# Replanning a two-engine split: LayerNorm work and evictions that may go to either VectorE or ScalarE, with new scheduler constants

## The chip, the cores and the metric

The kernel runs on one core of one Trainium2 chip. The metric is the device time of one execution in microseconds (us). TensorE (PE in the profile) does matmuls, VectorE (DVE) and ScalarE (ACT) do element-wise work and copy PSUM to SBUF ("evictions"), GpSimd (POOL) small things, SyncE (SP) issues DMA.

## The reference, cut to what matters

One block on x of 2048 positions × 512 features, bf16: a modulated LayerNorm; sliding, dilated local attention (32 heads of 16, window 8, dilation 2) with a residual; a second modulated LayerNorm; a third LayerNorm and an MLP *along the positions* (2048 → 1792 → 2048) with a residual.

```python
h = layernorm(x) * (1 + ca) + sa
x = x + ga * attention(h, wqkv, wo)
h = layernorm(x) * (1 + cb) + sb
u = gelu(einsum('bsd,sf->bdf', layernorm(h), w1) + b1)
x = x + gb * (einsum('bdf,fs->bds', u, w2) + b2).transpose(0, 2, 1)
```

The MLP mixes positions, so its first matmul needs the third LayerNorm, `h3`, of *every* position before it can end, and the second matmul needs all of the first.

## The kernel before

Positions come in 4 chunks of 512, each of 4 tiles of 128. A chunk goes: statistics of x, normalise (`n_sb`), transpose (`hT`), project (`q`, `k`, `v`), multiply q by shifted k (`prod`), softmax, multiply by v (`pv`), output projection plus x (`xx`), statistics, normalise (`h`), affine, statistics again (`st6c`), normalise into `h3`. The first MLP matmul runs in levels: chunks 0 and 1, then chunk 2, then chunk 3, the partial sums parked in SBUF in between. They are parked in the buffer of the projection weights, so the last projection must be over first.

The program is not written in execution order. It is a graph of operations, each with a modelled duration, and a list scheduler in Python orders it once, at build time. Some operations carry alternatives, and the scheduler picks the engine. The kernel stamps this order on the instructions, and in the traces each engine ran *its* list in it (e5 below shows an eviction between two normalisations because that is where it stood).

```python
class _Graph:
    XLAT = 0.12            # modelled hand-over between two engines, us
    ...
    def schedule(self):
        ...
            for i in avail:
                o = ops[i]
                fin = [(max(ready_time(o, e), eng_free.get(e, 0.0)) + d, e, d) for (e, d, _) in o.alts]
                best_fin = min(fin)[0]
                for f_, e, d in fin:
                    if f_ <= best_fin + 0.05:
                        per_eng.setdefault(e, []).append((f_ - d, o, d))
        ...
def copy2(dst, src_fn, n, bf16_src, ...):     # evictions: hT, lsb, a2sb, o_sb, parked MLP sums
    alts = [("act", _t_act(n), fa)]
    if FLEX:
        alts.append(("dve", (0.12 + 0.00052 * n) if bf16_src else _t_tt1(n), fd))
    return G.add_any(alts, ...)
# fixed before: statistics of x and h -> VectorE; normalise x -> VectorE;
# normalise h, evict q/k/v, evict xx with its statistics -> ScalarE
add("dve", 0.72, f, reads=[("xx", st)], writes=[("mv", b, sl)], name=f"ln1s{st}")
# ... cut
order = G.schedule()
for o in order:
    o.fn()
```

## Time and profile before

256.71 us, median of 6 runs (256.01 to 258.49). The head of the profile's page: busy time by engine, then the span in 40 slices of 6.35 us (busy tenths; PEclk is the clock that TensorE was granted).

```profile
span 254.0 us, 3475 instructions
PE 211.2 (83%) x1295; PEld 93.2 (37%) x1295; DVE 178.0 (70%) x271; ACT 125.0 (49%) x234; POOL 5.8 (2%) x32
PE   0199946994889735787879989999999999999993
DVE  2479998999999999979997798627820044444543
ACT  2035645653687854658774758887696500000000
PEclk9999997999599985589999999999999999999999
```

VectorE is full from 16 to about 130 us while TensorE has holes; from about 131 us TensorE is full. The windows view has the same in us: window, its length, then busy time (and instructions) of each engine, the granted clock, and at the end the share and the GB/s of the DMA engines.

```profile
60.00:80.00 20.00, 15.54 (x120) 7.11 (x117) 19.40 (x29) 13.33 (x29) 0.00 (x0) 0.83 0.73 99
80.00:100.00 20.00, 12.09 (x85) 4.53 (x83) 19.44 (x25) 12.42 (x21) 0.90 (x2) 0.83 0.43 63
131.50:170.00 38.50, 37.71 (x238) 15.18 (x238) 28.00 (x41) 26.83 (x58) 0.00 (x0) 1.00 0.64 125
170.00:201.00 31.00, 30.99 (x144) 13.84 (x142) 11.58 (x23) 21.97 (x37) 0.00 (x0) 1.00 0.46 133
```

The order of columns is PE, PE weight load, DVE, ACT, POOL. And some groups of instructions (engine, operation, output <- input, shapes, count | busy us, mean ns of one):

```profile
L140 DVE TENSOR_SCALAR n_sb<-xx,mv,rs 128x512 bf16<-128x512 bf16 x16 | 5.8, 406 | 0.2 <-ACT rs L140 0.2
L140 ACT ACTIVATE h<-xx,nb,rs 128x512 bf16<-128x512 bf16 x16 | 11.7, 803 | 0.9 <-DVE nb L140 0.9
L140 ACT ACTIVATE q_sb<-psA,bqkv 128x512 bf16<-128x512 f32 x16 | 10.9, 683 | 4.3 <-PE psA L140 4.3
L140 ACT ACTIVATE xx<-psW 128x512 bf16<-128x512 f32 x16 | 9.5, 594 | 6.9 <-PE psW L140 6.9
```

The three ScalarE lines have two, one and no per-partition pointer operands (scale or bias read from a column in SBUF): 803, 683, 594 ns; the first also reads bf16 from SBUF, where the others read f32 from PSUM. So ScalarE pays twice what VectorE pays for a normalisation, but less for a plain f32 eviction (`o_sb`: 593 against 687 ns; the bf16 eviction `hT` is the other way round, 592 against 417).

Last, three moments, from the timeline (start, length): the first MLP matmul, the last normalisation into `h3`, and the first matmul of the second MLP product (MLP2). How many instructions are merged into one line depends on the window that was asked for.

```profile
131.53 1.02 PE L140 MATMUL psA<-h,wst 128*128 128x512 bf16 x4 [0.72 <-ACT v_c L140]
183.57 2.92 ACT L140 ACTIVATE h<-h,nb,rs 128x512 bf16<-128x512 bf16 x4
201.35 3.84 PE L140 MATMUL psA<-wg,wst 128*128 128x512 bf16 x17 [0.36 <-DMA wst<-in_B_w_dram]
```

### The profile page before, as it was taken

How to read it: one execution, taken by the hardware profiler on the slowest of the kernel's cores; microseconds unless marked ns; L12 is line 12 of the kernel's file. 1: busy time of each engine (PE TensorE's matmuls, PEld its weight loads, DVE VectorE, ACT ScalarE, POOL GpSimd, SP SyncE). 2: the span in 40 equal slices, each digit the busy share in tenths (PEclk: the TensorE clock that was granted, in tenths of full speed). 3: DMA queues.
4: the chain of work that ended last, by engine and by line, in shares of the span. 5: the costliest groups of instructions: out<-in, count | busy, mean ns of one | idle time of the engine just before them, and what ended most of it. 6: DMA issues, size and time to landing. Idle time of an engine off the chain costs nothing.

```text
span 254.0 us, 3475 instructions
## 1 busy us (share of the span) xinstructions
PE 211.2 (83%) x1295; PEld 93.2 (37%) x1295; DVE 178.0 (70%) x271; ACT 125.0 (49%) x234; POOL 5.8 (2%) x32
## 2 busy tenths in 40 slices
PE   0199946994889735787879989999999999999993
PEld 0164413441344311243423433444444444444441
DVE  2479998999999999979997798627820044444543
ACT  2035645653687854658774758887696500000000
POOL 4000000010000100000000000000000000000000
PEclk9999997999599985589999999999999999999999
DMA  6994069796950049800009993122444966666311
GB/s 236 383 306 152 0 118 218 167 166 115 146 78 0 3 89 141 106 4 0 0 0 165 147 271 89 41 83 83 126 124 122 278 202 203 203 205 200 120 41 41
DMA packets 46596, 32.87 MB, mean 129 GB/s; under 512 B 2036, under 2 KB 45556, under 8 KB 46580
## 3 DMA queue, kind: packets, MB, share of 16 engines
q1 hardware_dynamic: 45984, 31.60, 53.8%
q10 hardware_dynamic: 596, 1.06, 1.1%
q8 instruction: 10, 0.16, 0.3%
q14 instruction: 6, 0.05, 0.1%
HBM read 22.03 MB, written 2.10 MB: 95 GB/s over the span
## 4 chain that ended last, share of the span: by engine, by line
PE 59%; DVE 17%; DMA 14%; issue 4%; ACT 3%; SPq 1%; ACTq 0%; DVEq 0%; POOLq 0%
PE psA L140 43%; DVE pv L140 7%; PE psT L140 7%; PE psW L140 4%; DMA wst<-in_B_w_dram 4%; DMA b_t<-in_B_b_dram 4%; DMA vD<-v_c 4%; DMA wst<-in_w_mod_dram 2%; ACT h L140 2%; PE psO L140 2%; PE psL L140 2%; DVE h L140 2%; DVE prod L140 1%; SPq L140 1%; PE psX L140 1%
## 5 line engine op out<-in xcount | busy, mean ns | idle before, releaser
L140 PEld LDWEIGHTS <-wst 128*128 128x128 bf16 x448 | 43.1, 98 | 56.4 <-issue 3.7
L140 PE MATMUL psA<-hT,wg 128*128 128x512 bf16 x192 | 49.1, 398 | 3.0 <-ACT v_c L140 1.2
L140 PE MATMUL psA<-wg,wst 128*128 128x512 bf16 x224 | 48.5, 379 | 0.4 <-DMA wst<-in_B_w_dram 0.4
L140 DVE SCALAR_TENSOR_TENSOR h<-psA,b2col,gb_bc 128x512 f32<-128x512 f32 x16 | 12.0, 751 | 41.1 <-PE psA L140 41.1
L140 PE MATMUL psA<-h,wst 128*128 128x512 bf16 x152 | 37.8, 380 | 1.5 <-DMA wst<-in_B_w_dram 0.8
L140 DVE TENSOR_TENSOR pv<-a2sb,vD 128x2048 bf16<-128x2048 bf16 x32 | 37.7, 1217 | 0.0
L140 DVE TENSOR_TENSOR prod<-q_sb,k_c 128x4096 bf16<-128x4096 bf16 x16 | 36.0, 2285 | 0.4 <-PE psL L140 0.4
L140 PEld LDWEIGHTS <-wg 128*128 128x128 bf16 x240 | 23.2, 117 | 28.5 <-issue 12.5
L140 PE MATMUL psW<-woq,o_sb 128*128 128x512 bf16 x64 | 20.0, 443 | 0.9 <-ACT xx L140 0.8
L140 PE MATMUL psO<-pv,stack 128*32 128x512 bf16 x128 | 12.3, 432 | 8.9 <-DVE pv L140 6.2
L140 PE MATMUL psT<-h,wst 128*128 128x512 bf16 x72 | 18.0, 380 | 0.0
L140 DVE BATCH_NORM_STATS2 st<-xx 128x6 f32<-128x512 bf16 x16 | 10.7, 672 | 4.5 <-DMA xx<-in_A_x_dram 4.5
L140 PE MATMUL psL<-prod,group 128*32 128x512 bf16 x128 | 9.9, 398 | 4.8 <-DVE prod L140 4.8
L140 ACT ACTIVATE v_c<-psA,bqkv 128x512 bf16<-128x512 f32 x16 | 10.8, 685 | 6.0 <-PE psA L140 5.8
L140 ACT ACTIVATE k_c<-psA,bqkv 128x512 bf16<-128x512 f32 x16 | 10.9, 681 | 5.2 <-PE psA L140 5.2
L140 ACT ACTIVATE q_sb<-psA,bqkv 128x512 bf16<-128x512 f32 x16 | 10.9, 683 | 4.3 <-PE psA L140 4.3
L140 ACT ACTIVATE xx<-psW 128x512 bf16<-128x512 f32 x16 | 9.5, 594 | 6.9 <-PE psW L140 6.9
L140 ACT ACTIVATE h<-h,nb,rs 128x512 bf16<-128x512 bf16 x16 | 11.7, 801 | 2.0 <-DVE nb L140 2.0
L140 ACT ACTIVATE h<-xx,nb,rs 128x512 bf16<-128x512 bf16 x16 | 11.7, 803 | 0.9 <-DVE nb L140 0.9
L140 ACT ACTIVATE o_sb<-psO 128x512 bf16<-128x512 f32 x11 | 6.5, 593 | 11.2 <-PE psO L140 11.2
L140 DVE TENSOR_TENSOR h<-h,xx 128x512 bf16<-128x512 f32 x16 | 11.1, 692 | 0.6
L140 PE MATMUL psT<-ident,n_sb 128*128 128x128 bf16 x64 | 7.2, 271 | 4.4 <-DVE n_sb L140 3.1
(94 smaller groups left out, 200.2 us busy)
## 6 DMA issues: line engine op xcount, KB each, us to landing
vD<-v_c SPq DMA_DIRECT2D x64, 130.0 KB, 5.0
wst<-in_B_w_dram SPq DMA_DIRECT2D x8, 896.0 KB, 4.9
wst<-in_B_w_dram SPq DMA_DIRECT2D x7, 512.0 KB, 5.3
wst<-in_B_w_dram SPq DMA_DIRECT2D x14, 256.0 KB, 2.8
xx<-in_A_x_dram SPq DMA_DIRECT2D x4, 512.0 KB, 11.0
wst<-in_w_mod_dram SPq DMA_DIRECT2D x4, 512.0 KB, 6.1
out_dram<-h SPq DMA_DIRECT2D x16, 128.0 KB, 1.7
wg<-in_A_wqkv_dram SPq DMA_DIRECT2D x1, 1536.0 KB, 9.4
```

What stands on the lines that cost most here:

```text
L140: r = fn(*a, **k)
```

## The change

The intent is to take work off VectorE: LayerNorm statistics, normalisations and projection evictions get an alternative on the other engine, and the scheduler adds 1 us to VectorE's finish time when it compares the two. The modelled hand-over goes from 0.12 to 0.3 us. Four small groups of start-up operations are moved by hand after the scheduling, and four weight loads go to GpSimd's DMA queue.

```diff
-    XLAT = 0.12
+    XLAT = 0.3                 # (set from the argument XLAT = 30)
+    EBIAS = {}                 # (set to {"dve": 1.0} from DBIAS = 100)
-                best_fin = min(fin)[0]
+                best_fin = min(f_ + self.EBIAS.get(e, 0.0) for f_, e, d in fin)
                 for f_, e, d in fin:
-                    if f_ <= best_fin + 0.05:
+                    if f_ + self.EBIAS.get(e, 0.0) <= best_fin + 0.05:
# ...
+    def ln_stats(...):         # bn_stats on VectorE, or on ScalarE:
+        def fa():
+            # with eviction
+            nc.scalar.activation(evac_dst, x, ACT.Identity, accum_out=sums_ap[:, 0:1])
+            nc.scalar.activation(mv_ap[:, 0:1], sums_ap[:, 0:1], ACT.Identity, scale=1.0 / D)
+            nc.scalar.activation(junk[:], evac_dst, ACT.Square, scale=-1.0, bias=mv_ap[:, 0:1],
+                                 accum_out=mv_ap[:, 1:2])
+            # ... (without eviction: the same in another order)
+        alts = [("dve", d_dve, fd), ("act", d_act, fa)] if FLEX else [("dve", d_dve, fd)]
+    def ln_norm(...):          # tensor_scalar on VectorE, or activation on ScalarE
+        alts = [("dve", _t_ts(D), fd), ("act", _t_act(D, 2), fa)] if FLEX else [("act", _t_act(D, 2), fa)]
# ... q/k/v evictions: [("act", ...)] + [("dve", _t_tt1(C), fdv)]
# ... one small VectorE op per chunk (nb1) added before the first normalisation, three (mean, msq, ve) removed
+                q=nc.gpsimd if li == 0 and fc >= NWS else None)
# ...
     order = G.schedule()
+    move(("modcols", "modcols_cp"), "ln1n3")
+    move(("tr0_0", "hT0_0", "hT0_1", "tr0_1"), "modcols", before=True)
+    move(("biascols", "biascols_cp"), "w_scale")
+    move(("hT0_2", "hT0_3"), "tr0_1")
```

More of the change, by code (lines that the diff above doesn't have):

```diff
@@ L126, in schedule @@
         return order
+_CUR = [None]
 class _EngProxy:
@@ L143, in wrapped @@
                 self._tc.stamp_issue_order_token(ins, self._token)
+                if _CUR[0] and hasattr(r, "annotate"):
+                    r.annotate(_CUR[0])
             return r
@@ L210 @@
     FLEX: int = 1,
+    DBIAS: int = 100,
+    XLAT: int = 30,
 ):
@@ L214 @@
     G.WIN = WIN / 100.0
+    G.EBIAS = {"dve": DBIAS / 100.0}
+    G.XLAT = XLAT / 100.0
     SB = C // 4
@@ L309 @@
     sums = [T([P, TPC, 2], F32, f"sums{i}") for i in range(2)]
-    mean2 = [T([P, TPC], F32, f"mean2_{i}") for i in range(2)]
-    msq2 = [T([P, TPC], F32, f"msq2_{i}") for i in range(2)]
-    ve2 = [T([P, TPC], F32, f"ve2_{i}") for i in range(2)]
+    sums1 = [T([P, TPC, 2], F32, f"sums1_{i}") for i in range(2)]
+    sums3 = [T([P, TPC, 2], F32, f"sums3_{i}") for i in range(2)]
+    nb1 = [T([P, TPC], F32, f"nb1_{i}") for i in range(2)]
+    st6b = [T([P, TPC, 6], F32, f"st6b_{i}") for i in range(2)]
+    mv2 = [T([P, TPC, 2], F32, f"mv2_{i}") for i in range(2)]
     lv2 = [T([P, TPC], F32, f"lv2_{i}") for i in range(2)]
@@ L339, in copy2, with dma, ln_stats, fd @@
         return G.add_any(alts, reads=reads, writes=writes, name=name)
-    def dma(out_ap, in_ap, nbytes, reads, writes, name):
-        return add("sp", 0.65, lambda: nc.sync.dma_start(out_ap, in_ap), reads=reads, writes=writes, name=name,
+    def dma(out_ap, in_ap, nbytes, reads, writes, name, q=None):
+        return add("sp", 0.65, lambda: (q or nc.sync).dma_start(out_ap, in_ap), reads=reads, writes=writes, name=name,
                    bytes_=nbytes)
+    def ln_stats(src_fn, evac_dst, st6_ap, mv_ap, sums_ap, reads, writes, name):
+        def fd():
+            x = src_fn()
+            if evac_dst is not None:
+                nc.vector.tensor_copy(evac_dst, x)
+                x = evac_dst
+            nc.vector.bn_stats(st6_ap, x)
+            nc.vector.bn_aggr(mv_ap, st6_ap)
+            if evac_dst is not None:
+                nc.vector.tensor_scalar(mv_ap[:, 1:2], mv_ap[:, 1:2], float(D), None, op0=ALU.mult)
+        def fa():
+            x = src_fn()
+            if evac_dst is not None:
+                nc.scalar.activation(evac_dst, x, ACT.Identity, accum_out=sums_ap[:, 0:1])
+                nc.scalar.activation(mv_ap[:, 0:1], sums_ap[:, 0:1], ACT.Identity, scale=1.0 / D)
+                nc.scalar.activation(junk[:], evac_dst, ACT.Square, scale=-1.0, bias=mv_ap[:, 0:1],
+                                     accum_out=mv_ap[:, 1:2])
+            else:
+                nc.scalar.activation(junk[:], x, ACT.Identity, scale=1.0 / D, accum_out=mv_ap[:, 0:1])
+                nc.scalar.activation(junk[:], x, ACT.Square, scale=-1.0, bias=mv_ap[:, 0:1], accum_out=sums_ap[:, 1:2])
+                nc.scalar.activation(mv_ap[:, 1:2], sums_ap[:, 1:2], ACT.Identity, scale=1.0 / D)
+        d_dve = 0.72 + (_t_tt1(D) if evac_dst is not None else 0.0)
+        d_act = 2 * _t_act(D) + 0.2 + 0.75
+        alts = [("dve", d_dve, fd), ("act", d_act, fa)] if FLEX else [("dve", d_dve, fd)]
+        return G.add_any(alts, reads=reads, writes=list(writes), name=name)
@@ L345, with ln_norm, fd, fa @@
+    def ln_norm(dst, src, mean_ap, rs_ap, nb_ap, reads, writes, name):
+        def fd():
+            nc.vector.tensor_scalar(dst, src, mean_ap, rs_ap, op0=ALU.subtract, op1=ALU.mult)
+        def fa():
+            nc.scalar.activation(dst, src, ACT.Identity, scale=rs_ap, bias=nb_ap)
+        alts = [("dve", _t_ts(D), fd), ("act", _t_act(D, 2), fa)] if FLEX else [("act", _t_act(D, 2), fa)]
+        return G.add_any(alts, reads=reads, writes=writes, name=name)
     G.pk = -20.0
@@ L467, in build_mod_rows, with rstd @@
         mod_row(5, 2, lambda ps: nc.vector.tensor_copy(gb_bc[:], ps[:]), "gb", 0.7, ["gb_bc"])
-    def rstd(var_ap, lv_t, rs_t, eps, reads, key, name):
+    def rstd(var_ap, lv_t, rs_t, eps, reads, key, name, scale=1.0):
         def f():
-            nc.scalar.activation(lv_t[:], var_ap, ACT.Ln, bias=epscol[:, 0:1] if eps else 0.0)
+            nc.scalar.activation(lv_t[:], var_ap, ACT.Ln, scale=scale, bias=epscol[:, 0:1] if eps else 0.0)
             nc.scalar.activation(rs_t[:], lv_t[:], ACT.Exp, scale=-0.5)
@@ L482, in build_chunk @@
             st = ch * TPC + sl
-            def f(st=st, sl=sl):
-                nc.vector.bn_stats(st6[b][:, sl, :], xx[:, st, :])
-                nc.vector.bn_aggr(mv[b][:, sl, :], st6[b][:, sl, :])
-            add("dve", 0.72, f, reads=[("xx", st)], writes=[("mv", b, sl)], name=f"ln1s{st}")
+            ln_stats(lambda st=st: xx[:, st, :], None, st6[b][:, sl, :], mv[b][:, sl, :], sums1[b][:, sl, :],
+                     [("xx", st)], [("mv", b, sl)], f"ln1s{st}")
         rstd(mv[b][:, :, 1], lv1[b], rs1[b], True, [("mv", b, sl) for sl in range(TPC)] + ["consts"], ("rs1", b),
              f"rstd1_{ch}")
+        add("dve", 0.12, lambda: nc.vector.scalar_tensor_tensor(nb1[b][:], mv[b][:, :, 0], -1.0, rs1[b][:],
+                                                               op0=ALU.mult, op1=ALU.mult),
+            reads=[("rs1", b)] + [("mv", b, sl) for sl in range(TPC)], writes=[("nb1", b)], name=f"ln1b{ch}")
         for sl in range(TPC):
             st = ch * TPC + sl
-            def f(st=st, sl=sl):
-                nc.vector.tensor_scalar(n_sb[b][:, sl, :], xx[:, st, :], mv[b][:, sl, 0:1], rs1[b][:, sl:sl + 1],
-                                        op0=ALU.subtract, op1=ALU.mult)
-            add("dve", _t_ts(D), f, reads=[("xx", st), ("rs1", b), ("mv", b, sl)], writes=[("n_sb", 0, sl)],
-                name=f"ln1n{st}")
+            ln_norm(n_sb[b][:, sl, :], xx[:, st, :], mv[b][:, sl, 0:1], rs1[b][:, sl:sl + 1], nb1[b][:, sl:sl + 1],
+                    [("xx", st), ("rs1", b), ("nb1", b), ("mv", b, sl)], [("n_sb", 0, sl)], f"ln1n{st}")
         G.pk = (ch - 1) * 100 + RK[4] + 1
@@ L548, in f, with fdv @@
                     nc.scalar.activation(v_c[b][:, j, PAD:PAD + C], psA[a][:, 0:C], ACT.Identity, bias=bqkv[:, g:g + 1])
-            add("act", _t_act(C, 1), f, reads=[("psA", a), "bqkv"], writes=[(("q", "k", "v")[t], b, j)],
-                name=f"ev{ch}_{t}{j}")
+            def fdv(t=t, j=j, a=a):
+                g = 4 * t + j
+                dst = (q_sb[b][:, j, :], k_c[b][:, j, PAD:PAD + C], v_c[b][:, j, PAD:PAD + C])[t]
+                if t == 0:
+                    nc.vector.tensor_scalar(dst, psA[a][:, 0:C], DH ** -0.5, bqkv[:, g:g + 1], op0=ALU.mult, op1=ALU.add)
+                else:
+                    nc.vector.tensor_scalar(dst, psA[a][:, 0:C], bqkv[:, g:g + 1], None, op0=ALU.add)
+            alts = [("act", _t_act(C, 1), f)] + ([("dve", _t_tt1(C), fdv)] if FLEX else [])
+            G.add_any(alts, reads=[("psA", a), "bqkv"], writes=[(("q", "k", "v")[t], b, j)], name=f"ev{ch}_{t}{j}")
         if ch == 0:
@@ L659, in build_chunk @@
                 writes=["psW"], name=f"wo{st}")
-            def f(sl=sl, st=st):
-                nc.scalar.activation(xx[:, st, :], psW[:], ACT.Identity, accum_out=sums[b][:, sl, 0:1])
-                nc.scalar.activation(junk[:], xx[:, st, :], ACT.Square, scale=float(D) ** -0.5,
-                                     accum_out=sums[b][:, sl, 1:2])
-            add("act", 2 * _t_act(D) + 0.2, f, reads=["psW"], writes=[("xx", st), ("sums", b, sl), "junk"],
-                name=f"x1ev{st}")
-        def f():
-            nc.vector.tensor_scalar(mean2[b][:], sums[b][:, :, 0], 1.0 / D, None, op0=ALU.mult)
-            nc.vector.tensor_tensor(msq2[b][:], mean2[b][:], mean2[b][:], op=ALU.mult)
-            nc.vector.scalar_tensor_tensor(ve2[b][:], sums[b][:, :, 1], EPS, msq2[b][:], op0=ALU.add, op1=ALU.subtract)
@@ L672, in build_chunk @@
-        add("dve", 0.3, f, reads=[("sums", b, sl) for sl in range(TPC)], writes=[("ve2", b)], name=f"ln2a{ch}")
-        rstd(ve2[b][:], lv2[b], rs2[b], False, [("ve2", b)], ("rs2", b), f"rstd2_{ch}")
-        add("dve", 0.12, lambda: nc.vector.scalar_tensor_tensor(nb2[b][:], mean2[b][:], -1.0, rs2[b][:], op0=ALU.mult,
-                                                               op1=ALU.mult),
-            reads=[("rs2", b), ("ve2", b)], writes=[("nb2", b)], name=f"ln2b{ch}")
+            ln_stats(lambda: psW[:], xx[:, st, :], st6b[b][:, sl, :], mv2[b][:, sl, :], sums[b][:, sl, :],
+                     ["psW"], [("xx", st), ("mv2", b, sl)], f"x1ev{st}")
@@ L677, in build_chunk @@
+        rstd(mv2[b][:, :, 1], lv2[b], rs2[b], True, [("mv2", b, sl) for sl in range(TPC)], ("rs2", b), f"rstd2_{ch}",
+             scale=1.0 / D)
+        add("dve", 0.12, lambda: nc.vector.scalar_tensor_tensor(nb2[b][:], mv2[b][:, :, 0], -1.0, rs2[b][:],
+                                                               op0=ALU.mult, op1=ALU.mult),
+            reads=[("rs2", b)] + [("mv2", b, sl) for sl in range(TPC)], writes=[("nb2", b)], name=f"ln2b{ch}")
         for sl in range(TPC):
             st = ch * TPC + sl
-            add("act", _t_act(D, 2),
-                lambda sl=sl, st=st: nc.scalar.activation(h2[b][:, sl, :], xx[:, st, :], ACT.Identity,
-                                                          scale=rs2[b][:, sl:sl + 1], bias=nb2[b][:, sl:sl + 1]),
-                reads=[("xx", st), ("nb2", b), ("rs2", b)], writes=[("h2", b, sl)], name=f"t{st}")
+            ln_norm(h2[b][:, sl, :], xx[:, st, :], mv2[b][:, sl, 0:1], rs2[b][:, sl:sl + 1], nb2[b][:, sl:sl + 1],
+                    [("xx", st), ("nb2", b), ("rs2", b), ("mv2", b, sl)], [("h2", b, sl)], f"t{st}")
@@ L689, in build_chunk @@
         for sl in range(TPC):
-            def f(sl=sl):
-                nc.vector.bn_stats(st6c[b][:, sl, :], h2[b][:, sl, :])
-                nc.vector.bn_aggr(mv3[b][:, sl, :], st6c[b][:, sl, :])
-            add("dve", 0.72, f, reads=[("h2", b, sl)], writes=[("mv3", b, sl)], name=f"ln3s{ch}_{sl}")
+            ln_stats(lambda sl=sl: h2[b][:, sl, :], None, st6c[b][:, sl, :], mv3[b][:, sl, :], sums3[b][:, sl, :],
+                     [("h2", b, sl)], [("mv3", b, sl)], f"ln3s{ch}_{sl}")
         rstd(mv3[b][:, :, 1], lv3[b], rs3[b], True, [("mv3", b, sl) for sl in range(TPC)], ("rs3", b), f"rstd3_{ch}")
@@ L699, in build_chunk @@
             st = ch * TPC + sl
-            add("act", _t_act(D, 2),
-                lambda sl=sl, st=st: nc.scalar.activation(h3[:, st, :], h2[b][:, sl, :], ACT.Identity,
-                                                          scale=rs3[b][:, sl:sl + 1], bias=nb3[b][:, sl:sl + 1]),
-                reads=[("h2", b, sl), ("nb3", b), ("rs3", b)], writes=[("h3", st)], name=f"h3_{st}")
+            ln_norm(h3[:, st, :], h2[b][:, sl, :], mv3[b][:, sl, 0:1], rs3[b][:, sl:sl + 1], nb3[b][:, sl:sl + 1],
+                    [("h2", b, sl), ("nb3", b), ("rs3", b), ("mv3", b, sl)], [("h3", st)], f"h3_{st}")
     for ch_ in range(NCH):
@@ L734 @@
             w1p = wst[w][:, 0:nst, :]
-            dma(w1p, w1_view[:, s_lo:s_hi, fc * EW:(fc + 1) * EW], P * nst * EW * 2, [], [("wst", w)], f"ld_w1_{li}_{fc}")
+            dma(w1p, w1_view[:, s_lo:s_hi, fc * EW:(fc + 1) * EW], P * nst * EW * 2, [], [("wst", w)], f"ld_w1_{li}_{fc}",
+                q=nc.gpsimd if li == 0 and fc >= NWS else None)
             for fl in range(EW // P):
@@ L794, with move @@
     order = G.schedule()
+    def move(names, anchor, before=False):
+        nonlocal order
+        ops_ = [o for o in order if o.name in names]
+        order = [o for o in order if o.name not in names]
+        at = next(i for i, o in enumerate(order) if o.name == anchor) + (0 if before else 1)
+        order[at:at] = ops_
+    move(("modcols", "modcols_cp"), "ln1n3")
+    move(("tr0_0", "hT0_0", "hT0_1", "tr0_1"), "modcols", before=True)
+    move(("biascols", "biascols_cp"), "w_scale")
+    move(("hT0_2", "hT0_3"), "tr0_1")
     if DUMP:
@@ L801 @@
     for o in order:
+        _CUR[0] = o.name if DUMP else None
         o.fn()
+    _CUR[0] = None
 _INS = ['A_x', 'A_wqkv', 'A_wo', 'B_x', 'B_w1', 'B_b1', 'B_w2', 'B_b2', 'c', 'w_mod']
```

## The prediction

> **What bounds the kernel now.** The windows view splits the 254.0 us span into three. (1) To 15.8 us: start-up, waiting for loads. The first projection runs at 16.5 us. (2) 16 to 131.5 us: attention, where VectorE is busy 22.9 of 24.2, 18.3 of 20, 19.4 of 20, 19.4 of 20, 17.6 of 19.9 and 11.4 of 11.6 us. ScalarE is busy only 12.4, 11.7, 13.3, 12.4, 13.8, 9.4 there, TensorE about 90 of 115. The MLP cannot start before the last projection (its buffer is reused) and h3 of the second chunk; its first matmul is at 131.5 us. (3) From 131.5 us to the end TensorE is saturated (37.7 of 38.5, 31.0 of 31.0, 48.5 of 53 with the output tail). So the time is set by when TensorE saturates, and that is VectorE's queue in stage 2.
>
> **What the change does.** It lets the static scheduler put LayerNorm statistics, normalisations and projection evictions on either engine, and handicaps VectorE by 1 us in the choice. From the groups by form: a statistic costs VectorE 0.80 us of pace (0.67 + 0.18, overlapped) and would cost ScalarE about 1.9 us (0.6 + 0.63 plus two accumulator reads of 0.19 and a small op of 0.2: an estimate from the post-attention statistics). A normalisation costs 0.34 us against 0.73 us. The Trainium skill, "ScalarE: Activation LUTs" (What ACT_TABLE_LOAD costs) puts about 93 ns on each per-partition pointer operand; the trace agrees: 0.59, 0.685, 0.80 us with none, one, two.
>
> In stage 2 some 24 us of VectorE work can move (12 statistics of x, 12 normalisations, up to 8 statistics of h, about 15 evictions). ScalarE has about 35 us idle and pays about twice as much. Balance comes near 10 to 12 us moved. Waits between the two engines eat some; I count 7 us of earlier saturation. TensorE must do the same work in less time; its idle there (about 25 us) suffices, and fewer gaps may remove part of the half-clock stretches (mean clock 0.75 to 0.83 between 60 and 120 us).
>
> Start-up: transposes move ahead of the column matmuls, bias columns behind them. The chain is still the 1 MB w_mod load (about 11.7 us), column matmuls, bias matmuls, weight scaling, projection: 0.5 us gained. Four w1 loads leave the blocked SP queue for GpSimd's: it removes the 0.76 us wait at 150.5 us, no more. Stage 3 keeps its matmuls (MLP2 48.5 us unchanged), and the chunk tails (normalise, affine, statistics, h3) shorten, so saturation should hold.
>
> **Predicted: 248 us, range 241 to 254.5.** Faster by over 2%: 0.70; within 2%: 0.25; slower: 0.05.
>
> **What would show it.** First MLP matmul near 124 us instead of 131.5; VectorE total down from 178 to about 165, ScalarE up from 125 to about 150; statistics and normalisations appearing as ScalarE activations in the groups; first projection near 16 us; time from first MLP matmul to end unchanged within 2 us; clock nearer 1 between 60 and 120 us.
>
> **What would make it wrong.** ScalarE statistics of 1.9 us sit in order in front of projection evictions, and with two projection banks TensorE then stalls, so ScalarE becomes the new limiter. TensorE could get gaps in stage 3 if chunk 3's h3 (ready at 186.5 us, used from 186 us) does not come earlier by as much as the rest. The GpSimd-issued loads could land late beside VectorE ("SBUF - State Buffer" of the skill, on the shared port); no run here shows that yet.

## The result, and the profile after

250.13 us, median of 8 runs (249.49 to 251.34), against 257.97 us for the kernel before over 16 runs. The ratio is 0.9716, 95% interval 0.9687 to 0.9744. Ratios here are the mean time of one kernel's runs over that of the other's in the same rounds, so not quite the ratio of the medians quoted. The profiled execution of before was the fastest of its 16 (256.01 us), that of after an ordinary one (249.84), so the profiles show 6.0 of the 7.8 us. The page after:

```profile
span 248.0 us, 3499 instructions
PE 209.5 (84%) x1295; PEld 91.3 (37%) x1295; DVE 166.0 (67%) x239; ACT 146.3 (59%) x297; POOL 11.6 (5%) x36
PE   0389976998989235996889999999899999999992
DVE  2369999899999998899955899116700044444442
ACT  5576577859875778797996788768876300000000
PEclk9999995899999957797999999999999999999998
```

VectorE lost 12.0 us of work and ScalarE gained 21.3 us. Most of the 12.0 is not LayerNorm work. In the groups, VectorE's plain evictions (`hT`, `o_sb`, `a2sb`, `lsb`, the parked sums), which could change engine before too, go from 27 with 17.0 us to 13 with 8.7 us. Of the new alternatives, 8 of the 32 statistics of x and h and 6 of the 16 normalisations of x left VectorE, but 6 normalisations of h, one eviction of `xx` with its statistics and two projection evictions came to it. The three moments after:

```profile
127.64 3.62 PE L144 MATMUL psA<-h,wst 128*128 128x512 bf16 x16
177.66 1.51 ACT L144 ACTIVATE h<-h,nb,rs 128x512 bf16<-128x512 bf16 x2
194.63 9.67 PE L144 MATMUL psA<-wg,wst 128*128 128x512 bf16 x44 [0.47 <-DMA wst<-in_B_w_dram]
```

The last `h3` ends 7.3 us earlier (186.5 to 179.2 us), and MLP2 starts 6.7 us earlier. The first MLP matmul moved by only 3.9 us.

There is a new hole. In the windows view, after, TensorE does 8.6 us of work between 80 and 100 us, where it did 12.1 before:

```profile
60.00:80.00 20.00, 18.95 (x147) 8.12 (x143) 19.59 (x23) 15.17 (x33) 1.00 (x1) 1.00 0.57 87
80.00:100.00 20.00, 8.61 (x68) 2.82 (x67) 18.16 (x32) 16.32 (x32) 0.98 (x1) 0.73 0.74 100
```

The timeline shows what TensorE waited for first: the eviction of `o_sb`, which stood in ScalarE's list behind the eviction of logits, four normalisations and a `v` eviction.

```profile
85.80 0.98 PE L144 MATMUL psO<-pv,stack 128*32 128x512 bf16 x8 [4.71 <-ACT o_sb L144]
80.42 1.00 ACT L144 ACTIVATE lsb<-psL 128x1024 bf16<-128x1024 f32 x1
81.76 2.93 ACT L144 ACTIVATE h<-xx,nb,rs 128x512 bf16<-128x512 bf16 x4 [0.34 <-DVE nb L144]
84.59 0.67 ACT L144 ACTIVATE v_c<-psA,bqkv 128x512 bf16<-128x512 f32 x1
85.17 0.58 ACT L144 ACTIVATE o_sb<-psO 128x512 bf16<-128x512 f32 x1
```

Over the two windows together TensorE does the same work as before, 27.6 us: what it gains in the first is given back in the second, to a queue that is longer now. Is the relief of VectorE what paid at all?

### The profile page after: what moved, and what is told of

Read it like the earlier page. It is cut to its first block, busy times and chain, and to the rows that moved or that the text cites. A ratio compares the mean times of both kernels' runs of the same rounds, so it can differ in the third digit from the quotient of the medians.

```text
span 248.0 us, 3499 instructions
## 1 busy us (share of the span) xinstructions
PE 209.5 (84%) x1295; PEld 91.3 (37%) x1295; DVE 166.0 (67%) x239; ACT 146.3 (59%) x297; POOL 11.6 (5%) x36
## 4 chain that ended last, share of the span: by engine, by line
PE 63%; DVE 21%; ACT 8%; DMA 3%; issue 3%; DVEq 0%; ACTq 0%
PE psA L144 44%; PE psW L144 7%; PE psT L144 6%; DVE pv L144 6%; DVE prod L144 4%; ACT h L144 3%; DVE h L144 3%; PE psL L144 2%; PE psO L144 2%; DMA wst<-in_B_w_dram 2%; PE psX L144 2%; DVE st6c L144 2%; DVE st L144 1%; DMA xx<-in_A_x_dram 1%; ACT junk L144 1%
## 5 line engine op out<-in xcount | busy, mean ns | idle before, releaser
L144 PE MATMUL psA<-hT,wg 128*128 128x512 bf16 x192 | 52.6, 417 | 6.4 <-DVE k_c L144 2.2
L144 PE MATMUL psA<-h,wst 128*128 128x512 bf16 x152 | 37.1, 380 | 0.0
L144 PE MATMUL psO<-pv,stack 128*32 128x512 bf16 x128 | 11.4, 425 | 9.7 <-ACT o_sb L144 6.1
L144 PE MATMUL psW<-woq,o_sb 128*128 128x512 bf16 x64 | 18.3, 409 | 0.3 <-ACT o_sb L144 0.3
L144 PE MATMUL psT<-ident,n_sb 128*128 128x128 bf16 x64 | 6.9, 268 | 10.4 <-ACT n_sb L144 6.6
L144 ACT ACTIVATE junk<-xx,mv 128x512 bf16<-128x512 bf16 x19 | 13.7, 722 | 0.6
L144 ACT ACTIVATE k_c<-psA,bqkv 128x512 bf16<-128x512 f32 x15 | 10.2, 679 | 4.7 <-PE psA L144 4.5
L144 DVE CAST wg<-psA 128x512 bf16<-128x512 f32 x6 | 4.1, 680 | 10.8 <-PE psA L144 10.7
L144 ACT ACTIVATE h<-xx,nb,rs 128x512 bf16<-128x512 bf16 x14 | 10.3, 802 | 1.4 <-DVE nb L144 1.4
L144 DVE BATCH_NORM_STATS2 st<-xx 128x6 f32<-128x512 bf16 x12 | 8.0, 670 | 4.4 <-DMA xx<-in_A_x_dram 4.4
L144 PEld LDWEIGHTS <-n_sb 128*128 128x128 bf16 x64 | 5.4, 121 | 12.8 <-ACT n_sb L144 7.0
```

The lines of the kernel that those rows point to most:

```text
L144: r = fn(*a, **k)
```

## The experiments

Three theories. **Theory 1**, the prediction's: the LayerNorm work that left VectorE is the gain. **Theory 2**: the scheduler's constants are the gain, and the new alternatives are not needed. **Theory 3**: every edit makes the scheduler draw another order for everything, and the order is the gain, whatever VectorE's total. All outputs were correct. Times are medians of 4 runs in experiments 1 to 8 and of 6 in 9 to 12; the kernel before was at 257.26, 257.32 and 257.28 us in the three groups of four. Submitted together: e1 to e4, e5 to e8, e9 to e12; each ratio is against before in the same rounds, while after was timed in rounds of its own.

### e1: the two constants alone, on the kernel before

```diff
-    XLAT = 0.12
+    XLAT = 0.3
+    EBIAS = {"dve": 1.0}      # and used in the choice, as in the change; nothing else
```

> The kernel before, with only the scheduler's two constants of the change: hand-over latency 0.3 us instead of 0.12, and the 1 us handicap of VectorE for the evictions that could already go to either engine. No LayerNorm statistic, normalisation or projection eviction may move. Theory 1 (the gain is VectorE work moved by the new alternatives): VectorE total stays near 175 us and the time within 2 us of before, 255 to 258 us. Theory 2 (the new scheduler constants alone do it, the alternatives are not needed): 248 to 252 us, VectorE total down by 5 to 8 us through evictions alone. Theory 3 (any new static order shifts the time by a few us): anything between 250 and 260, with no relation to VectorE's total.

Measured: 250.97 us, ratio 0.9749 (0.9715 to 0.9782). VectorE's total is 167.9 us: 24 evictions went from VectorE to ScalarE, 6 the other way. Almost the whole gain is there without one line of the new alternatives: the interval overlaps that of the change (0.9687 to 0.9744). The time is that of Theory 2; VectorE's relief is larger than the 5 to 8 us I expected.

```profile
PE 210.3 (84%) x1295; PEld 91.7 (37%) x1295; DVE 167.9 (67%) x253; ACT 132.9 (53%) x252; POOL 9.7 (4%) x32
```

### e2: the hand-over constant alone

```diff
-    XLAT = 0.12
+    XLAT = 0.3
```

> The kernel before with only the hand-over latency of the plan at 0.3 us. VectorE's work is the same to within 2 us. Theory 1: within 2 us of before. Theory 2: faster by 2 to 5 us[...]. Theory 3: a shift either way; the plan's own end is 13 us later than that of before (259.8 against 246.6), so if the plan is now true the kernel is slower, 256 to 262 us.

Measured: 268.71 us, ratio 1.0424 (1.0382 to 1.0466), with VectorE at 178.9 us, the work of before. A more careful constant alone made it 11 us slower, outside every range that I had written. Part of that is in waits of TensorE for w1, of which before had 0.8 us: in the group of the first MLP product 8.7 us of idle, 5.5 us of it for those loads.

```profile
L140 PE MATMUL psA<-h,wst 128*128 128x512 bf16 x152 | 39.9, 396 | 8.7 <-DMA wst<-in_B_w_dram 5.5 <-ACT h L140 3.2
```

### e3: the change without its new alternatives

```diff
-        alts = [("dve", d_dve, fd), ("act", d_act, fa)] if FLEX else ...   # statistics
+        alts = [("act", d_act, fa)] if evac_dst is not None else [("dve", d_dve, fd)]
# normalisations: x on VectorE, h on ScalarE; q/k/v evictions: ScalarE only
```

> The kernel after, with the new alternatives taken back: statistics of x and h on VectorE, normalisation of x on VectorE, of h on ScalarE, post-attention eviction and statistics and projection evictions on ScalarE, as before. Handicap, latency, start-up moves, GpSimd queue and the new form of the variance stay. Theory 1: the gain goes, 254 to 258 us, with VectorE's total back to 172 or more. Theory 2: the gain stays, 248 to 252 us. Theory 3: either, unrelated to VectorE's total.

Measured: 254.41 us, ratio 0.9879 (0.9845 to 0.9912). It lies between: taking the alternatives away from the change costs 4.3 us of its median, though e1, which never had them, is at 251.0. VectorE: 170.1 us. e3 and e1 have the same constants and the same fixed engines for the LayerNorm work; they differ in the start-up moves, the GpSimd loads and the form of the variance, and are 3.4 us apart. So edits that move little work can shift the time by nearly as much as the alternatives.

### e4: the change without the handicap

```diff
-    DBIAS: int = 100,
+    DBIAS: int = 0,
```

> The kernel after with the handicap of VectorE at 0 instead of 1 us; the alternatives stay. Theory 1: the scheduler already spreads work by finish time, so most of the gain stays, 249 to 253 us, but VectorE's total is higher than after's 166. Theory 2: the gain goes, 255 us or more, with VectorE's total above 175 us as it takes evictions and normalisations from ScalarE.

Measured: 261.33 us, ratio 1.0148 (1.0108 to 1.0189). VectorE's total rises to 190.6 us. The alternatives without the handicap *load* VectorE, because most of the operations that may now move are modelled shorter there, and the kernel is 4 us slower than before.

### e5 and e6: the engines alone, and the order alone

These two split e1. In e5 the order of before is kept, and after the scheduling 30 evictions are put on the engine that e1 chose. In e6 the order of e1 is kept, and the same 30 are put back.

```diff
     order = G.schedule()
+    for o in order:
+        want = 'act' if o.name in (24 names) else 'dve' if o.name in (6 names) else None   # e6: swapped
+        for (ae, ad, afn) in o.alts:
+            if ae == want:
+                o.eng, o.dur, o.fn = ae, ad, afn
```

> The order of instructions of before, kept as it is; only the engine of 30 evictions is changed in place, to the engines that the plan of e1 chose (24 from VectorE to ScalarE, 6 the other way). Theory 1a (the relief of VectorE is the gain, whatever the order): most of e1's gain is there, 251 to 254 us, VectorE near 168 us. Theory 3 (the order is the gain): within 2 us of before, 255 to 259 us.

> The order of e1, kept as it is; only the engines of the same 30 evictions are put back in place to what they were before. Theory 1a: the gain goes, 255 us or more, VectorE near 178. Theory 3: the gain stays, 250 to 253 us.

Measured: e5 259.54 us, ratio 1.0080 (1.0034 to 1.0127); e6 257.44 us, ratio 1.0002 (0.9972 to 1.0033). VectorE's totals were 167.6 and 177.2 us (e5, then e6):

```profile
PE 213.8 (83%) x1295; PEld 93.7 (37%) x1295; DVE 167.6 (65%) x253; ACT 132.5 (52%) x252; POOL 6.7 (3%) x32
PE 211.8 (83%) x1295; PEld 92.1 (36%) x1295; DVE 177.2 (69%) x271; ACT 123.6 (48%) x234; POOL 9.9 (4%) x32
```

e5 is just above Theory 3's range and e6 is in Theory 1a's: e5 refutes the relief alone and e6 the order alone. This is the sharpest result: taking 10.4 us off VectorE with the order kept is worth nothing (it is slightly slower), the new order with the old engines is worth nothing, and both together, in e1, are worth 2.5%.

Where part of e5's relief went can be read. The waits view of VectorE (who waited for whom, total us, times, longest), before and then e5:

```profile
DVE h L140 <- ACT h L140: 0.2, 1, 0.2
DVE h L140 <- ACT h L140: 7.5, 4, 4.0
```

One instance of the four, a short one (1.3 us; the longest, 4.0 us, is in chunk 3's tail at 178 us), before: ScalarE does four normalisations of `h` in a row, meanwhile VectorE evicts `o_sb` and goes on to the affine step at 85.67 us.

```profile
82.71 2.93 ACT L140 ACTIVATE h<-xx,nb,rs 128x512 bf16<-128x512 bf16 x4 [0.68 <-DVE nb L140]
84.79 0.68 DVE L140 CAST o_sb<-psO 128x512 bf16<-128x512 f32 x1
85.67 1.22 DVE L140 TENSOR_TENSOR h<-h,ab_bc 128x2048 bf16<-128x2048 bf16 x1 [0.20 <-ACT h L140]
```

In e5 the eviction sits on ScalarE, between the third and the fourth normalisation, since that is where it stood in the common order. VectorE is idle for it, and its affine step starts at 86.25 us, *later*:

```profile
82.81 2.22 ACT L140 ACTIVATE h<-xx,nb,rs 128x512 bf16<-128x512 bf16 x3 [0.68 <-DVE nb L140]
84.94 0.57 ACT L140 ACTIVATE o_sb<-psO 128x512 bf16<-128x512 f32 x1
85.42 0.80 ACT L140 ACTIVATE h<-xx,nb,rs 128x512 bf16<-128x512 bf16 x1
86.25 1.22 DVE L140 TENSOR_TENSOR h<-h,ab_bc 128x2048 bf16<-128x2048 bf16 x1 [1.27 <-ACT h L140]
```

### e7: the order of after, with the LayerNorm work put back

The same loop on the kernel after: statistics, normalisations and projection evictions on the engines of before, order and plain evictions kept.

> The order of after, kept as it is; only the statistics, normalisations and projection evictions are put back in place on the engines that they had before; the plain evictions stay where after has them. Some 19 items of VectorE work, about 11 us, come back. Prediction's step (the LayerNorm work moved off VectorE is what is gained): 4 to 8 us slower than after, 254 to 258 us. If the plain evictions and the order carry the gain: within 2 us of after, 248 to 252 us.

Measured: 259.13 us, ratio 1.0072 (1.0037 to 1.0106): 9.0 us slower than after's median, beyond the 4 to 8 us expected. But VectorE's total is 169.1 us: 3.1 us came back, not about 11, since the put-back returns work to both engines.

```profile
PE 209.5 (82%) x1295; PEld 90.8 (35%) x1295; DVE 169.1 (66%) x249; ACT 134.8 (52%) x264; POOL 21.7 (8%) x36
```

So of the 12.0 us that left VectorE, 3.1 us net belong to the new alternatives, and a loss of 9.0 us cannot be VectorE's load alone. Within *this* order the new alternatives are worth all of the gain. With e3 (4.3 us when the scheduler may plan again without them) this suggests how to value a part: an order fits the engines that it was planned for. One thing blurs e7: GpSimd's small copy of the k halo, which the next chunk's products read, took 11.7 us there instead of 1.4, while VectorE ran two-input multiplications back to back. First after, then e7:

```profile
50.91 1.38 POOL L144 COPY k_c<-k_c 128x64 bf16<-128x64 bf16 x1 [15.89 <-ACT k_c L144]
```

```profile
53.55 11.73 POOL L144 COPY k_c<-k_c 128x64 bf16<-128x64 bf16 x1 [17.17 <-ACT k_c L144]
56.82 8.03 DVE L144 TENSOR_TENSOR pv<-a2sb,vD 128x2048 bf16<-128x2048 bf16 x7
```

How much of the 9.0 us that is was not separated.

### e8: the handicap alone, on the kernel before

> The kernel before with only the handicap of VectorE of 1 us, the latency of the plan left at 0.12 us. If the handicap is the part that works: 249 to 253 us, as e1. If the two constants work only together: 255 us or more. The plan's own end is 242.9 us[...].

The edit is e1's without the XLAT line. Measured: 252.10 us, ratio 0.9798 (0.9767 to 0.9830). So the handicap alone brings most of it, and the hand-over constant, which alone cost 4.2%, cost nothing once the handicap was there. Three pairs differ in the handicap alone, and it paid in each: from before to e8 VectorE loses 10.6 us and the time 5.2; from e2 to e1 11.0 and 17.7; from e4 to after 24.6 and 11.2. Where the scheduler plans the order together with the relief, relief and gain go together; their sizes do not.

### e9: the change without its start-up moves

```diff
-    move(("modcols", "modcols_cp"), "ln1n3")
-    move(("tr0_0", "hT0_0", "hT0_1", "tr0_1"), "modcols", before=True)
-    move(("biascols", "biascols_cp"), "w_scale")
-    move(("hT0_2", "hT0_3"), "tr0_1")
```

> The kernel after without the four start-up moves (transposes ahead of the column matmuls, bias columns behind the weight scaling). Prediction: they are worth 0.5 us, so 0.2 to 1 us slower than after, with the first projection at 16.7 instead of 16.2 us. Rival: the order behind the start-up absorbs it and nothing changes, within 0.3 us.

Measured: 252.56 us, ratio 0.9818 (0.9791 to 0.9844), 2.4 us slower than after's median and 2.0 us slower than e10 of the same rounds; my 0.2 to 1 us was too little. The timeline of VectorE in e9 shows why:

```profile
12.28 0.17 DVE L144 COPY b1col<-psO 128x14 f32<-128x14 f32 x1 [4.92 <-PE psO L144]
12.78 0.15 DVE L144 SCALAR_TENSOR_TENSOR nb<-mv,rs 128x4 f32<-128x4 f32 x1
```

The new plan had put the bias columns' copy, which waits for a load, in front of the operation (`nb`) that ScalarE's first normalisation needs; VectorE's own first ones follow it at 12.85 us. VectorE stood 4.9 us, and the first projection ran at 17.7 us. Against the kernel before (16.5 us) the moves gain 0.3 us; against the *new* plan they repair 1.5 us.

### e10: the four loads back on the SP queue

```diff
-                q=nc.gpsimd if li == 0 and fc >= NWS else None)
+                q=None)
```

> The kernel after with the four w1 loads back on the SP queue. Prediction: they save one wait of TensorE of some 0.8 us, so 0.5 to 1.5 us slower than after. Rival: the loads of the third chunk pair wait for slots in front of the vD loads or behind them in the SP queue, and TensorE stalls longer, 2 us or more. Or: no difference, if the loads were early enough.

Measured: 250.56 us, ratio 0.9747 (0.9709 to 0.9785), which overlaps after's interval. The wait comes back in the group of the first MLP product (0.9 us, after: none), but the time does not resolve it.

```profile
L144 PE MATMUL psA<-h,wst 128*128 128x512 bf16 x152 | 37.1, 379 | 0.9 <-DMA wst<-in_B_w_dram 0.9
```

### e11 and e12: other plans for the same work

If the order matters this much, one can look for a better one. I replayed each candidate's order off the chip: every engine in its order, modelled durations, a hand-over of 0.12, 0.2 and 0.3 us, and averaged the three ends. Over the first ten measured kernels that replay at 0.2 us was off by 4 us (standard deviation) with a correlation of 0.69, so it only serves to choose; the chip decides. Of about 3,400 settings, two from the top:

```diff
# e11, against after                      # e12, against after
-    WIN: int = 25,                       # RK=(10, 20, 30, 40, 5): next chunk's LayerNorm and
+    WIN: int = 10,                       #   projections ahead of the rest in rank
-    LEVELS=(2, 3),                       # LEVELS=(1, 2, 3)
+    LEVELS=(1, 2, 3),                    # DBIAS = 60
-    DBIAS: int = 100,                    # XLAT = 35
+    DBIAS: int = 80,
```

> The kernel after with another plan: handicap 0.8 instead of 1.0 us, choice window 0.10 instead of 0.25 us, MLP in four levels (one per chunk) instead of three. No instruction's work changes except 14 more injections and parkings. If the plan is what limits, and a plan can be picked by replaying it with hand-overs of 0.12 to 0.3 us: 242 to 247 us. If the picked plan was luck of the replay: 248 to 254 us. The replay's error over the runs so far is 4 us.

> As e11, with handicap 0.6 us, latency of the plan 0.35 us, the next chunk's LayerNorm and projections ahead of the rest in rank, four levels. Same expectation, 242 to 247 us if plans can be picked so, else 248 to 256 us. A gap of TensorE of 11 us between 80 and 100 us in the trace of after (waits for the third projection's input) should shrink.

Measured: e11 **242.61 us**, ratio 0.9432 (0.9398 to 0.9465); e12 244.05 us, ratio 0.9471 (0.9439 to 0.9504). Both beat after and before. The page of e11:

```profile
span 240.6 us, 3558 instructions
PE 209.2 (87%) x1309; PEld 90.7 (38%) x1309; DVE 171.2 (71%) x259; ACT 141.6 (59%) x287; POOL 10.9 (5%) x36
PE   0287999999999776999826999999999999999991
DVE  2459999999999999999996999527400244444442
PEclk9999999999999997999985899999999999999999
```

VectorE has *more* work than in after (171.2, and 176.6 in e12, nearly the 178.0 of before). But it is busier in the middle: 59.0 of 60 us between 60 and 120 us, against 56.8 in after and 56.5 before; TensorE does 54.0 us of work there against 44.4 and 43.5, at a mean clock of 0.97 against 0.86 and 0.80. The hole of after between 80 and 100 us is mostly filled (15.1 us of TensorE work against 8.6); e11 has one of its own, at 120 to 132 us. The first MLP matmul runs at 93.6 us, inside the attention stage, and fills its holes: this plan has its last projection at 92.5 us, against 125.7 in after, and the MLP may begin then. Which of the settings did it was not tried one by one. The obvious rival to a better order is the split into four levels, which e11 and e12 share: it gives TensorE MLP work that needs chunk 0 alone.

## Why the prediction was right or wrong, point by point

The time was right: 248 us predicted, 250.1 measured, inside 241 to 254.5, and faster by over 2%, as given 0.70. Several steps of the reasoning were right, and two were not; that their errors left the sum near 248 is in part luck.

| run | us | DVE total | first MLP | last h3 ends | TensorE idle until then | MLP2 starts |
|---|---|---|---|---|---|---|
| before | 256.7 | 178.0 | 131.5 | 186.5 | 38.4 | 201.4 |
| after | 250.1 | 166.0 | 127.6 | 179.2 | 33.2 | 194.6 |
| e1 constants only | 251.0 | 167.9 | 115.5 | 179.6 | 34.9 | 197.1 |
| e2 hand-over only | 268.7 | 178.9 | 136.8 | 197.8 | 46.9 | 214.2 |
| e4 no handicap | 261.3 | 190.6 | 107.2 | 192.1 | 41.3 | 207.0 |
| e5 engines only | 259.5 | 167.6 | 131.4 | 188.9 | 38.2 | 203.9 |
| e6 order only | 257.4 | 177.2 | 119.4 | 186.7 | 38.8 | 202.5 |
| e11 other plan | 242.6 | 171.2 | 93.6 | 172.3 | 26.0 | 187.2 |
| e12 other plan | 244.1 | 176.6 | 93.6 | 173.5 | 27.8 | 189.2 |

All columns but the time are read from each profiled execution; the idle time is the end of the last `h3` less TensorE's busy time up to there in the windows view. In the rounds of the experiments before was at 257.3 us.

- **Sizes of what moves: the sums right, the parts not.** VectorE 166.0 (predicted about 165), ScalarE 146.3 (about 150), two of 48 projection evictions on VectorE, first projection at 16.2 us (near 16). But LayerNorm work and projection evictions make up 3.1 us net of VectorE's 12.0 (e7); plain evictions are most of the rest.
- **"ScalarE has about 35 us idle ... balance comes near 10 to 12 us moved": right as a sum, wrong as a reason.** e5 moved 10.4 us and gained nothing; e12 gained 5.3% with VectorE 1.4 us below before. What counted in e1, e5 and e6 was whether the order had been made for the assignment. In e5 ScalarE's idle time was of use only at the place in its list where the work landed.
- **"The time is set by when TensorE saturates", with the first MLP matmul as its mark: this step failed.** I expected it near 124 us and an unchanged rest. It came at 127.6, and the rest of the span became 2.1 us shorter: from the first projection to that moment after runs 29 more matmuls than before does (622 against 593). That TensorE is saturated from there on did hold in both, with 0.8 us of idle up to the last `h3`. In other plans it did not:

```profile
131.53:186.49 54.96, 54.20 (x314) 22.67 (x314) 39.43 (x64) 38.66 (x80) 0.00 (x0) 1.00 0.56 121
115.53:179.63 64.10, 55.13 (x302) 22.66 (x302) 41.90 (x70) 46.80 (x96) 0.00 (x0) 0.89 0.47 100
```

The second line is e1: its first MLP matmul comes 16 us earlier than before, but TensorE is then idle for 9.0 us of 64.1, and the gain is 6 us. In e4 it comes 24 us earlier, with 16.2 us of idle after it, for a loss of 4. The first MLP matmul marks no more than the last projection (129.3 us before, 106.9 in e4), which a plan can place early while attention work is left. The marks that hold in every row are TensorE's idle time up to the last `h3`, whose order is that of the times but for e5 (in part by construction, since the time is idle plus busy), and the last `h3` itself: MLP2 starts 14.9 to 17.5 us after it, which is the 70 matmuls of the last level (70 × 0.216 us = 15.1 us, the pace of warm matmuls in the trace; the first can start before the fourth tile of `h3` is done) and up to 2.4 us more. Whether chunk 3's chain or TensorE's own backlog sets that end is not shown: in before and after TensorE hardly waited.

- **The statistics and normalisations named as the gain: not needed.** e1 has none of them moved and is within 0.8 us of after. In the order of after they matter (e7); they are one way to a good plan, not the cause that I gave.
- **"ScalarE statistics sit in order in front of projection evictions": the risk came true in another place**, the 4.7 us wait for `o_sb` behind four normalisations.
- **Start-up, 0.5 us: mis-sized** for the moves themselves (2.0 to 2.4 us, e9), and 0.3 us against before.
- **Queue, 0.76 us: the wait did go** (none in the first MLP product after, 0.9 us in e10), but no gain in time is resolved (e10).
- **Clock: partly.** The mean between 60 and 120 us went from 0.80 to 0.86. The Trainium skill, "TensorE: Matmul & The Clock Gate" (What's actually happening), says that the clock is halved by default and full when TensorE has been busy; these runs agree in direction: TensorE's busy time in that window is 43.5 us before, 44.4 after and 54.0 in e11, which has 0.97.
- **Pointer operands:** the 93 ns each of the skill's page "ScalarE: Activation LUTs" agrees roughly with the 594, 683 and 803 ns above (89 and 120 ns; the second step also changes the source from PSUM to SBUF).

What stays open: why one order is several us better than another was followed only at single waits (e2, e5, e9, the hole of after), not as a whole; and which of the settings of e11 and e12, four levels above all, carries their gain. Nor was the part of the loads tested: on the chain that ended last the pages put 14% of the span on DMA before (4% on `vD<-v_c`, the copies of v) and 3% after, and VectorE's share there rose from 17% to 21%.

## What to carry to other kernels

Here, moving work off the busiest engine paid only together with a new order for all engines; test both halves apart, in place, before you credit either. Then count what moved by kind: the total alone hid that most of it was not the work the change was about. In a statically scheduled kernel any edit redraws the order: here kernels with the same outputs ranged from 242.6 to 268.7 us, so a part's worth read from one such edit is not its own, and a search over plans, with one more level for the MLP, brought the gain over before to twice that of the change. Take as the mark of progress the idle time of the limiting engine up to the last input of the last dependent stage, not the moment at which that engine starts to look full.

## What the Trainium skill lacked or had wrong

- "SBUF — State Buffer" (Who interferes with whom) says that a VectorE instruction with two SBUF inputs contends with a GpSimd instruction that reads SBUF. It does not say how long a GpSimd copy can lose in a row: in e7 a 128x64 copy that takes 0.24 us at its shortest (before) was on record for 11.7 us, over the rest of two VectorE multiplications and seven more. That the port was the cause is argued from the page, not shown.
- The same page warns that GpSimd-issued loads are starved while VectorE runs in its two-port modes. Here four such loads of 512 KB took a median of 5.6 us from issue to landing (7.1 us for the seven of that size from SP in e10), and 0.9 to 1.0 us each on GpSimd; TensorE never waited for them in the first MLP product of after. Whether VectorE was in such a mode then was not looked at, so this does not show the page wrong.
- "ScalarE: Activation LUTs" gives no cost for the accumulator output. In these traces it is a separate instruction of 0.19 us each, two per ScalarE statistic.
- No page gives a rule for the hand-over between engines to put into a static plan. With 0.12 us the plan of before ended 7.4 us ahead of its profile (246.6 against 254.0); with 0.3 us the plan of e1 ended 2.0 us ahead (247.8 against 249.8), that of e2 7.0 us ahead (259.8 against 266.8), and that of after 3.3 us behind (251.3 against 248.0). The plans' ends are those that the kernels print when built with their DUMP switch.
